# Transposes inside the key products, grad_out products in M's PSUM buffers, and two norms of the turn on ScalarE

## The chip, the cores and the metric

The kernel runs on one NeuronCore of a Trainium2 chip. The core has five engines that run their own instruction streams in order and meet at semaphores: TensorE (PE, matrix products; its weight loads are shown apart as PEld), VectorE (DVE), ScalarE (ACT), GpSimd (POOL) and SyncE (SP), which here only issues transfers. ACT and POOL issue some transfers too. The metric is the device time of one execution in microseconds, taken as the median of several.

## The reference

One forward and one backward pass of a pre-LN block over x of 2048 rows and 640 columns (bf16), with 32 heads of 20 columns and an MLP 1728 wide:

```python
phi = lambda t: where(t > 0, t + 1, exp(t)) + 1e-6
q, k, v = split(layernorm(x) @ wqkv)               # 32 heads
kv, z   = phi(k).T @ v, sum(phi(k))                # per head
h       = x + ((phi(q) @ kv) / (phi(q) @ z + 1e-6)) @ wo
hn      = layernorm(h)
out     = h + (silu(hn @ w1) * (hn @ w3)) @ w2
```

The kernel returns `out` and the gradients of x, wqkv, wo, w1, w3 and w2 for a given `grad_out` (B_x enters as a constant and isn't used in the result).

## The kernel before

Everything is cut into 16 tiles of 128 rows (`ST`), and 640 columns into 5 chunks of 128 (`DT`); a product over 640 columns is done in two halves of 320. Nothing is planned by a scheduler: the pools run under a manual schedule, so on each engine and each transfer queue the instructions stand in the order in which the Python code calls them.

**The first stage** (lines 432 to 513) loads x, normalises each tile in place in `x_sb` (bn_stats on DVE, the inverse root as a `pow` on POOL at L154, the norm itself on DVE at L160, or on ACT at L165 for tiles 10, 12 and 14), and turns it into `pqT`: tiles 0 to 7 by TensorE transposes (`p1_tr`, L254) that ACT copies out of PSUM (L256), tiles 8 to 15 by transfers on SP (L247). The loop over t then makes, for tile t, the key product of ten matmuls (`p1_mm`, L260) into a PSUM buffer `big`, of which there are two; `phi` takes it out with an Exp and a Relu on ACT (L277, L278) and two more steps on DVE (`rest`, L281 and L282) that are held back and called later by `phi_rest`. Key tile after key tile the loop also does the statistics of later tiles (`stat_of`), their norms (`norm_of`), four query products (`q_tile`), four products with grad_out (`ghh_chunk`, L371, which use one of the two `big` buffers), and the products of M = phi(k)^T x (`m_part`, L402, PSUM tags `m` and `tr`). In front of all that stand 44 products of a constant tile of ones (`warm`, L441), whose result nothing reads.

**The turn** (the `run(...)` at lines 801 to 809) stands between the end of the attention part and the MLP. `f2_half(t, j)` makes one half of h for tile t (L586, for t < 4 and j = 1 with a first product L584 that adds x), takes it out of PSUM (on DVE at L591 for j = 0, on ACT at L589 for j = 1) and takes its statistics on DVE; the second half also does the aggregation (L150), adds epsilon (L153) and asks POOL for the inverse root (L154). `f2_hn(t)` normalises on DVE (L160) into `hn`, and `f2_ht(t)` transposes it on TensorE (L677) and copies it out on ACT (L678). `mlp_ghh` is one more chunk of grad_out's products, taken out on ACT (L391).

**The backward loop** (L1112 to L1143) makes, for each row tile t, the 54 products of `b_ghn` (L1000): weights are 27 chunks of `ggb[t // 2]`, which holds two row tiles and has two buffers. The first 28 of the 54 products use chunks 0 to 13 and the operand `w13a`, the other 26 use chunks 14 to 26 and `w13b`. `load_gg` loads a `ggb` on the SP queue in two transfers: chunks 0 to 13 at even t, chunks 14 to 26 at odd t, for the pair of tiles that begins at the next even t. Within t the ACT queue issues a transposing transfer of the gradient of tile t - 1 (`b_gT`, L1037), then for t up to 10 one of `wo` or `kvT` (L1133). `b_gr(t - 2)` (L1057) uses the transposed gradient.

Of the kernel before, what the change touches and what calls it, by code (L numbers as in the profile page):

```python
# [9 lines left out]
P = 128  # L10
# [14 lines left out]
HD = D // 2  # L25
# [30 lines left out]
def kernel(  # L56
# [73 lines left out]
    class Stats:  # L130
# [31 lines left out]

        def norm_act(self, out, src, t):

            A.activation(out=out, in_=src, func=AF.Identity, bias=self.nb[t][:, 1:2], scale=self.rs[:, t:t + 1])  # L165

        def bias(self, t):
            nb = self.nb[t] = cp.tile([P, 2], F32, name="nb", bufs=4)
            G.tensor_tensor(out=nb[:, 0:1], in0=self.mv[:, t, 0:1], in1=self.rs[:, t:t + 1], op=ALU.mult)
            G.tensor_tensor(out=nb[:, 1:2], in0=zero[:], in1=nb[:, 0:1], op=ALU.subtract)  # L170

    ln1, ln2 = Stats("ln1"), Stats("ln2")

# [7 lines left out]
    def load_wq(a, b):  # L181
        dma(out=wqkv[:, :, a * HD:b * HD], in_=wq_v[:, :, a * HD:b * HD])

    def load_x(a, b):
        dma(out=x_sb[:, a:b, :], in_=xS[:, a:b, :])

    load_x(1, 2)
    A.activation(sg[:], zero[:], AF.Exp)
    load_wq(2, 3)
    load_wq(3, 4)  # L190
    load_x(2, 3)
    load_x(3, 4)
    load_x(4, 8)

# [40 lines left out]
    Z = cp.tile([P, DT], F32, name="Z")  # L235

    XT_DMA = 8
    WARM = 44

    def on_act(t):  # L240
        return t > XT_DMA and t % 2 == 0

    def p1_norm(t):
        xn = x_sb[:, t, :]
        (ln1.norm_act if on_act(t) else ln1.norm)(xn, xn, t)
        if t >= XT_DMA:
            dmaT(out=pqT[:, :, t * P:(t + 1) * P], in_=xn)  # L247

    def p1_tr(t, parts=((0, DT),)):
        xn = x_sb[:, t, :]  # L250
        for a, b in parts:
            tr = ps.tile([P, DT, P], BF16, name="tr", bufs=2)
            for c in range(a, b):
                T.transpose(tr[:, c, :], xn[:, c * P:(c + 1) * P], ident[:])  # L254

            A.copy(out=pqT[:, a:b, t * P:(t + 1) * P], in_=tr[:, a:b, :])  # L256

    def p1_half(acc, t, n0):
        for c in range(DT):
            T.matmul(acc, lhsT=pqT[:, c, t * P:(t + 1) * P], rhs=wqkv[:, c, n0:n0 + HD], start=(c == 0),  # L260
                     stop=(c == DT - 1))

    def p1_mm(t, n0):
        acc = ps.tile([P, 2, 512], F32, name="big", bufs=2)
        for j in range(2):
            p1_half(acc[:, j, 0:HD], t, n0 + j * HD)
        return acc

    def two(ap):
        return ap.rearrange("p (j n) -> p j n", j=2)  # L270

    held = []

    def phi(acc, dst, then=None):

        mq, rq = (p1.tile([P, D], BF16, name=n, bufs=b) for n, b in (("mq", 3), ("rq", 3)))
        A.activation(two(mq[:]), acc[:, :, 0:HD], AF.Exp)  # L277
        A.activation(two(rq[:]), acc[:, :, 0:HD], AF.Relu)  # L278

        def rest():  # L280
            V.tensor_scalar(out=mq[:], in0=mq[:], scalar1=1.0, scalar2=1e-6, op0=ALU.min, op1=ALU.add)  # L281
            V.tensor_tensor(out=dst, in0=mq[:], in1=rq[:], op=ALU.add)  # L282
            if then is not None:
                then()
        held.append(rest)

    def phi_rest(keep=0):
        while len(held) > keep:
            held.pop(0)()
# [13 lines left out]

    def q_tile(t):
        q_home(t)
        phi(p1_mm(t, 0), pqs[t])

    dz = {}

# [119 lines left out]
    def load_w2T(a, b):  # L429
        dmaT(out=w2T[:, :, a:b], in_=B_w2[a:b, :])  # L430

    zero_pads()
    load_w2T(0, 2 * P)
    load_g2T(0)
    load_w2T(2 * P, 4 * P)
    load_x(8, 12)
    load_wq(0, 2)
    load_x(12, ST)
    warm = ps.tile([P, 512], F32, name="warm", tag="tr", bufs=2)
    for _ in range(WARM):  # L440
        T.matmul(warm[:, 0:P], lhsT=ones[:], rhs=ones[:], start=True, stop=True, skip_group_check=True)  # L441
    ln1.run(x_sb, 0, 1)
    ln1.part(x_sb, 1, 0)
    for a, b in ((0, 2 * P), (2 * P, D)):
        ln1.norm(x_sb[:, 0, a:b], x_sb[:, 0, a:b], 0)
    p1_tr(0, ((0, 2), (2, DT)))
    for t in (1, 2):
        if t == 1:
            ln1.part(x_sb, t, 1)
            p1_norm(t)  # L450
            ln1.run(x_sb, t + 1, t + 2)
        else:
            ln1.part(x_sb, t + 1, 0)
            p1_norm(t)
    ln1.part(x_sb, 3, 1)
    w13 = [go for c0, c1 in ((0, 2), (2, 4), (4, 5)) for go in load_w13(c0, c1)]
    w13 += [lambda: dma(out=w1[:, :, F:FP], in_=rows(B_w3)[:, :, F - FL:F])]

    def load_wo():
        dma(out=wo[:], in_=A_wo.rearrange("(c p) n -> p c n", p=P))  # L460

    trickle = {3: w13[0], 4: w13[1], 11: lambda: load_wq(4, 6), 12: w13[2], 14: w13[3], 15: load_wo}

    stat_of = {t: (t + 4,) for t in range(7)}
    stat_of.update({7: (11, 12), 8: (13,), 9: (14,), 10: (15,)})
    norm_of = {t: (t + 3,) for t in range(8)}
    norm_of.update({8: (11, 12), 9: (13,), 10: (14,), 11: (15,)})

    def xn_out(g, q):
        sl = slice(g * TPC, (g + 1) * TPC)  # L470
# [5 lines left out]

    outs = {6: ((group_out, 0),), 7: ((xn_out, 0, dma),), 10: ((group_out, 1), (xn_out, 1, dma)), 13: ((group_out, 2),)}

    QT = (5, 7, 9, 11)
    for t in range(ST):  # L480
        k = p1_mm(t, D)
        if t < 3:
            p1_tr(t + 1, ((0, 2), (2, DT)))
        for n in stat_of.get(t, ()):
            ln1.run(x_sb, n, n + 1)
            if on_act(n):
                ln1.bias(n)
        for n in norm_of.get(t, ()):
            if not on_act(n):
                p1_norm(n)  # L490
        phi_rest(t < 4)
        phi(k, pk_all[:, t, :])
        for n in norm_of.get(t, ()):
            if on_act(n):
                p1_norm(n)
# [12 lines left out]
        for f, *n in outs.get(t, ()):  # L508
            f(*n)
        if t in trickle:  # L510
            trickle[t]()
# [285 lines left out]
    def kv3():  # L797
# [129 lines left out]

    ggb = {}

    def load_gg(j, c0, c1):  # L930
        if c0 == 0:
            ggb[j] = ba.tile([P, NG, 2 * P], BF16, name="ggb", bufs=2)
        dma(out=ggb[j][:, c0:c1, :],
            in_=gg_d[c0 * P:c1 * P, j * 2 * P:(j + 1) * 2 * P].rearrange("(c p) w -> p c w", p=P))

    def gw2_tail():
# [175 lines left out]
    for t in range(ST):  # L1112
        g = b_ghn(t)

        def part():
            next(g, None)

        u = t - 2
        if 2 <= t <= ST - 3:
            load_gg(t // 2 + 1, *((FT, NG) if t % 2 else (0, FT)))  # L1120
        part()
        part()
        part()
        if t + 2 < ST:
            b_load(t + 2)
        if t >= 1:
            ln_rest.pop(t - 1)()
            if by_dma(t - 1):
                b_gT(t - 1)
            if t <= 2 * DT:  # L1130
                n = (t - 1) % DT
                dst, src = (woT, A_wo) if t <= DT else (kvN, kvT_d)
                A.dma_start_transpose(out=dst[:, :, n * P:(n + 1) * P], in_=src[n * P:(n + 1) * P, :])  # L1133
# [300 lines left out]
```

## Time and profile before

| what | value |
|---|---|
| median of 6 runs | 826.96 us (826.25 to 828.49) |
| the profiled execution: its time, its span | 827.03 us, 825.3 us |
| TensorE busy | 815.5 us, 99% of the span |
| DVE, ACT, POOL busy | 453.6, 319.0, 133.9 us |
| granted TensorE clock | 0.999 |
| first stage: first warm product, first key product | 1.12 us, 6.92 us |
| the turn: first f2_half to first MLP product | 88.54 us to 101.68 us |
| the backward loop: first and last tile start | 404.6 us, 532.3 us |

The span runs from the first to the last instruction of the program; the execution's own time is 1.7 us longer. A line of a timeline has start, duration, engine, source line, operation, what it writes and reads, and in brackets the idle time of the engine before it with what ended it. TensorE shows as busy nearly throughout, so the time can change only by what makes TensorE wait, by products added or taken away, and by what lies ahead of its first useful product.

### The profile page before, as it was taken

How to read it: one execution, taken by the hardware profiler on the slowest of the kernel's cores; microseconds unless marked ns; L12 is line 12 of the kernel's file. 1: busy time of each engine (PE TensorE's matmuls, PEld its weight loads, DVE VectorE, ACT ScalarE, POOL GpSimd, SP SyncE). 2: the span in 40 equal slices, each digit the busy share in tenths (PEclk: the TensorE clock that was granted, in tenths of full speed). 3: DMA queues.
4: the chain of work that ended last, by engine and by line, in shares of the span. 5: the costliest groups of instructions: out<-in, count | busy, mean ns of one | idle time of the engine just before them, and what ended most of it. 6: DMA issues, size and time to landing. Idle time of an engine off the chain costs nothing.

```text
span 825.3 us, 14190 instructions
## 1 busy us (share of the span) xinstructions
PE 815.5 (99%) x5524; PEld 523.2 (63%) x5551; DVE 453.6 (55%) x960; ACT 319.0 (39%) x609; POOL 133.9 (16%) x196
## 2 busy tenths in 40 slices
PE   8999999999999999999999999999999999999998
PEld 5677644555555555777777777777777777555554
DVE  7859897899898566300057777772681545200000
ACT  5865787665655666011121222222212334211111
POOL 2335333323222212100001111110220000000000
PEclk9999999999999999999999999999999999999999
DMA  9899999696494455999878898358995788885771
GB/s 247 221 314 212 257 237 280 206 233 169 123 220 132 148 197 167 209 258 258 224 166 181 186 218 199 64 107 177 267 218 95 164 196 168 216 203 131 164 170 38
DMA packets 318338, 157.58 MB, mean 191 GB/s; under 512 B 235456, under 2 KB 311456, under 8 KB 318272
## 3 DMA queue, kind: packets, MB, share of 16 engines
q1 hardware_dynamic: 286256, 120.65, 63.4%
q0 software_dynamic: 7376, 24.81, 8.8%
q10 hardware_dynamic: 24640, 11.23, 6.8%
q8 instruction: 43, 0.70, 0.4%
q14 instruction: 23, 0.19, 0.1%
HBM read 48.15 MB, written 51.46 MB: 121 GB/s over the span
## 4 chain that ended last, share of the span: by engine, by line
PE 96%; DMA 2%; SPq 1%; ACT 0%; issue 0%; DVE 0%; POOL 0%; ACTq 0%
PE mm L371 20%; PE job L1198 19%; PE ghn L1000 14%; PE gxn L1356 8%; PE o L766 7%; PE gw L955 7%; PE big L260 3%; PE gwo L1085 3%; PE dkv L1302 3%; PE gr L1057 3%; PE macc L402 3%; PE at L586 2%; PE mm L260 1%; DMA pqT<-pql 1%; DMA g2T<-in_grad_out_dram 1%; PE dkv L1230 1%
## 5 line engine op out<-in xcount | busy, mean ns | idle before, releaser
L1198 PE MATMUL job<-gb,hnN 128*128 128x432 bf16 (+2 forms) x656 | 117.0, 342 | 0.0
L1000 PEld LDWEIGHTS <-ggb 128*128 128x128 bf16 x864 | 84.5, 98 | 32.8
L1198 PEld LDWEIGHTS <-hnN 128*128 128x128 bf16 x656 | 63.6, 98 | 53.4
L371 PE MATMUL mm<-pqT,w 128*128 128x512 bf16 x395 | 92.8, 379 | 0.4
L371 PEld LDWEIGHTS <-w 128*128 128x128 bf16 x540 | 52.5, 98 | 62.9 <-issue 0.8
L1202 ACT CAST obs<-job 128x432 bf16<-128x432 f32 (+3 forms) x61 | 29.3, 480 | 123.1 <-PE job L1198 120.7
L766 PE MATMUL o<-w,hhT 128*128 128x320 bf16 x448 | 67.6, 299 | 0.1
L1000 PE MATMUL ghn<-w13a,ggb 128*128 128x320 bf16 x448 | 63.5, 299 | 0.0
L1000 PE MATMUL ghn<-w13b,ggb 128*128 128x320 bf16 x416 | 61.4, 299 | 0.0
L371 PE MATMUL mm<-g2T,w2T 128*128 128x512 bf16 x229 | 58.9, 379 | 0.6
L766 PEld LDWEIGHTS <-hhT 128*128 128x128 bf16 x448 | 43.8, 98 | 23.6
L955 PE MATMUL gw<-g,hb 128*128 128x320 bf16 x416 | 56.8, 299 | 0.0
L1065 POOL TENSOR_TENSOR sz<-Zb,g_h 128x640 f32<-128x640 bf16 x16 | 20.2, 1261 | 199.3 <-DVE g_h L1063 199.3
L955 PEld LDWEIGHTS <-hb 128*128 128x128 bf16 x416 | 40.6, 98 | 16.0 <-issue 0.3
L1356 PE MATMUL gxn<-wqT,gT 128*128 128x320 bf16 x320 | 48.7, 299 | 0.0
L391 ACT CAST ghh<-mm 128x512 bf16<-128x512 f32 x48 | 28.2, 587 | 47.5 <-PE mm L371 42.0
L705 ACT ACTIVATE sig<-mm 128x512 bf16<-128x512 f32 x56 | 33.5, 598 | 27.8 <-PE mm L371 25.0
L1012 ACT ACTIVATE gs<-ghn 128x640 bf16<-128x640 f32 x16 | 11.2, 703 | 79.0 <-PE ghn L1000 79.0
L260 PE MATMUL big<-wqkv,pqT 128*128 128x320 bf16 x260 | 39.3, 299 | 1.8 <-DMA wqkv<-in_A_wqkv_dram 1.1
L371 PEld LDWEIGHTS <-w2T 128*128 128x128 bf16 x260 | 25.3, 98 | 24.6 <-issue 1.3
L260 PEld LDWEIGHTS <-pqT 128*128 128x128 bf16 x320 | 30.6, 98 | 14.6 <-ACT pqT L256 1.8
L1356 PEld LDWEIGHTS <-gT 128*128 128x128 bf16 x320 | 31.3, 98 | 12.2
(201 smaller groups left out, 1282.4 us busy)
## 6 DMA issues: line engine op xcount, KB each, us to landing
hh_d<-hhT SPq DMA_DIRECT2D x24, 256.0 KB, 2.6
gg_d<-gate POOLq DMA_DIRECT2D x24, 256.0 KB, 4.0
gg_d<-ghh POOLq DMA_DIRECT2D x24, 256.0 KB, 3.4
ggb<-gg_d SPq DMA_DIRECT2D x6, 896.0 KB, 5.8
ggb<-gg_d SPq DMA_DIRECT2D x6, 832.0 KB, 7.6
x_sb<-in_A_x_dram SPq DMA_DIRECT2D x7, 640.0 KB, 7.0
out_dram<-obs ACTq DMA_DIRECT2D x39, 108.0 KB, 3.0
ggb<-gg_d SPq DMA_DIRECT2D x2, 1728.0 KB, 13.4
```

Source lines behind the costliest of these rows:

```text
L260: T.matmul(acc, lhsT=pqT[:, c, t * P:(t + 1) * P], rhs=wqkv[:, c, n0:n0 + HD], start=(c == 0), stop=(c == DT - 1))
L371: T.matmul(acc[:], lhsT=w[:, c, fc * P:(fc + 1) * P], rhs=rhs[:, c, :], start=(c == 0), stop=(c == DT - 1))
L391: A.copy(out=ghh[n // 2][:, n % 2, :], in_=acc[:])
L402: T.matmul(macc[m][j][:, 0:n], lhsT=pk_all[:, t, m * P:(m + 1) * P], rhs=x_ext[:, t, j * HD:j * HD + n], start=(t == 0), stop=(t == ST - 1))
L705: A.activation(sig[:, i, :], gp[:], AF.Sigmoid)
L766: T.matmul(o2["ps"][:, 0:HD], lhsT=hhT[c][:, fc, i * P:(i + 1) * P], rhs=w2[:, fc, j * HD:(j + 1) * HD], start=(fc == 0), stop=(fc == FT - 1))
L955: T.matmul(acc[:, j, 0:HD], lhsT=hb[b][:, t, i * P:(i + 1) * P], rhs=g2[:, t, j * HD:(j + 1) * HD], start=(t == 0), stop=(t == ST - 1))
L1000: T.matmul(acc[:, j, 0:HD], lhsT=ggb[t // 2][:, k, lo:lo + P], rhs=rhs[:, j * HD:(j + 1) * HD], start=(k == 0), stop=(k == NG - 1))
L1057: T.matmul(gr[t][:, j, 0:HD], lhsT=ghT[t][:, c, :], rhs=wT2[:, c, j * HD:(j + 1) * HD], start=(c == 0), stop=(c == DT - 1))
L1198: T.matmul(acc[:, 0:n], lhsT=lhs[:, t, m * P:(m + 1) * P], rhs=rhs(t), start=(t == 0), stop=(t == ST - 1))
L1202: A.copy(out=ob, in_=acc[:, 0:n])
L1356: T.matmul(acc[:, j, 0:HD], lhsT=g, rhs=wqT[:, k, j * HD:(j + 1) * HD], start=(k == 0), stop=(k == 14))
```

## The change

In the first stage, tile 0 is only centred at first (its first 256 columns on DVE, the others on ACT with a bias of minus the mean); the scale is put into the Exp and Relu of its key and query products (`RAW = 1`), and `p1_scale` scales the tile in `x_sb` at t = 3. The transposes of tile t + 1 stand between the two halves of key product t, each tile with one copy. The warm products are 34, in M's buffers, and 8 more follow the transposes of tile 0. The loop's DVE work follows a written list (`v_steps`). Chunks of grad_out's products stand at t = 3 to 6 instead of 2 to 5 and use the two buffers `m`, so M's first products begin at t = 7. The first query product moves from t = 5 to t = 6. The load of x's tile 2 stands ahead of the second half of the key weights, that of tiles 8 to 11 ahead of w2's second part. The bias of ACT's norms is one POOL instruction instead of two. In the turn, the first half of tile 2 stands ahead of the second halves of tiles 0 and 1, and the norms of tiles 1 and 2 are done on ACT. In the backward loop the second half of each `ggb` is issued on the ACT queue, after `b_gT`.

```diff
         def norm_act(self, out, src, t):
-            A.activation(out=out, in_=src, func=AF.Identity, bias=self.nb[t][:, 1:2], scale=self.rs[:, t:t + 1])
+            A.activation(out=out, in_=src, func=AF.Identity, bias=self.nb[t][:, 0:1], scale=self.rs[:, t:t + 1])
         def bias(self, t):
-            nb = self.nb[t] = cp.tile([P, 2], F32, name="nb", bufs=4)
-            G.tensor_tensor(out=nb[:, 0:1], in0=self.mv[:, t, 0:1], in1=self.rs[:, t:t + 1], op=ALU.mult)
-            G.tensor_tensor(out=nb[:, 1:2], in0=zero[:], in1=nb[:, 0:1], op=ALU.subtract)
+            nb = self.nb[t] = cp.tile([P, 1], F32, name="nb", bufs=4)
+            G.tensor_scalar(out=nb[:], in0=self.mv[:, t, 0:1], scalar1=self.rs[:, t:t + 1], scalar2=-1.0, op0=ALU.mult,
+                            op1=ALU.mult)
...
     load_wq(2, 3)
+    load_x(2, 3)
     load_wq(3, 4)
-    load_x(2, 3)
     load_x(3, 4)
...
-    WARM = 44
+    WARM = 34
+    RAW = 1
...
+    def p1_scale(t):
+        xn = x_sb[:, t, :]
+        V.tensor_scalar(out=xn, in0=xn, scalar1=ln1.rs[:, t:t + 1], scalar2=None, op0=ALU.mult)
...
-    def p1_mm(t, n0):
+    def p1_mm(t, n0, between=None):
         acc = ps.tile([P, 2, 512], F32, name="big", bufs=2)
         for j in range(2):
             p1_half(acc[:, j, 0:HD], t, n0 + j * HD)
+            if j == 0 and between is not None:
+                between()
         return acc
...
+        kw = dict(scale=ln1.rs[:, t:t + 1]) if t < RAW else {}
+        A.activation(two(mq[:]), acc[:, :, 0:HD], AF.Exp, **kw)
+        A.activation(two(rq[:]), acc[:, :, 0:HD], AF.Relu, **kw)
...
     load_g2T(0)
+    load_x(8, 12)
     load_w2T(2 * P, 4 * P)
-    load_x(8, 12)
...
+    def warm_up(n):
+        warm = ps.tile([P, 512], F32, name="warm", tag="m", bufs=2)
+        for _ in range(n):
+            T.matmul(warm[:, 0:P], lhsT=ones[:], rhs=ones[:], start=True, stop=True, skip_group_check=True)
+    warm_up(WARM)
...
+    def center_first():
+        V.tensor_scalar(out=nmean[:], in0=ln1.mv[:, 0, 0:1], scalar1=-1.0, scalar2=None, op0=ALU.mult)
+        center(0, 0, 2 * P)
+        A.activation(out=x_sb[:, 0, 2 * P:], in_=x_sb[:, 0, 2 * P:], func=AF.Identity, bias=nmean[:, 0:1])
...
+    ln1.part(x_sb, 0, 0)
+    ln1.part(x_sb, 0, 1, center_first)
     p1_tr(0, ((0, 2), (2, DT)))
+    warm_up(8)
+    stat(1)
+    ln1.part(x_sb, 2, 0)
+    p1_norm(1)
+    ln1.part(x_sb, 2, 1)
+    ln1.part(x_sb, 3, 0)
+    p1_norm(2)
     ln1.part(x_sb, 3, 1)
+    ln1.part(x_sb, 4, 0)
+    p1_norm(3)
+    ln1.part(x_sb, 4, 1)
...
-    trickle = {3: w13[0], 4: w13[1], 11: lambda: load_wq(4, 6), 12: w13[2], 14: w13[3], 15: load_wo}
+    trickle = {4: w13[0], 5: w13[1], 11: lambda: load_wq(4, 6), 12: w13[2], 14: w13[3], 15: load_wo}
+    R = None
+    v_steps = {1: (R, ("N", 4)), 2: (("S", 5), R, ("N", 5)), 3: (("S", 6), R, ("N", 6), ("C", 0)),
+               4: (("S", 7), R, ("N", 7), ("S", 8)), 5: (R, ("N", 8), ("S", 9)), 6: (R, ("N", 9), ("S", 10)),
+               7: (("S", 11), R, R, ("A", 10), ("N", 11)), 8: (("S", 12), R, R, ("S", 13), ("A", 12)),
+               9: (("N", 13), R, ("S", 14)), 10: (R, R, ("S", 15), ("A", 14)), 11: (("N", 15), R)}
+    V_OPS = {"S": stat, "N": p1_norm, "C": p1_scale}
...
-    QT = (5, 7, 9, 11)
+    QT = (6, 7, 9, 11)
+    M0 = {7: (0, 1, 2), 8: (3, 4, 5)}
+    M0.update({t: (t - 3,) for t in range(9, ST)})
     for t in range(ST):
-        k = p1_mm(t, D)
-        if t < 3:
-            p1_tr(t + 1, ((0, 2), (2, DT)))
...
+        k = p1_mm(t, D, (lambda: p1_tr(t + 1)) if t + 1 < XT_DMA else None)
+        steps = v_steps.get(t, (R,) * len(held))
+        for step in steps:
+            if step is R:
+                held.pop(0)()
+            elif step[0] != "A":
+                V_OPS[step[0]](step[1])
+        phi(k, pk_all[:, t, :], t)
+        for step in steps:
+            if step is not R and step[0] == "A":
+                p1_norm(step[1])
         if t in QT:
             q_tile(QT.index(t))
-        if 2 <= t < 6:
-            ghh_chunk(t - 2, ps.tile([P, 2, 512], F32, name="gp", tag="big", bufs=2)[:, 0])
-            p1_tr(t + 2)
-        if t >= 3:
-            m_part(0, [t - 3])
+        if 3 <= t < 7:
+            ghh_chunk(t - 3, ps.tile([P, 512], F32, name="gp", tag="m", bufs=2))
+        m_part(0, M0.get(t, ()))
...
-    def f2_hn(t):
+    def f2_hn(t, on_act=False):
...
-        ln2.norm(hn[t][:], x_sb[:, t, :], t)
+        if on_act:
+            ln2.bias(t)
+            ln2.norm_act(hn[t][:], x_sb[:, t, :], t)
+        else:
+            ln2.norm(hn[t][:], x_sb[:, t, :], t)
...
-        (sig_table,), (f2_half, 0, 0), (f2_half, 1, 0), (f2_half, 0, 1), (f2_half, 1, 1), (f2_hn, 0), (mlp_ghh, 5),
-        (f2_half, 2, 0), (f2_hn, 1), (load_w2T, 10 * P, F), (f2_half, 2, 1), (f2_ht, 0), (f2_half, 3, 0), (f2_hn, 2),
+        (sig_table,), (f2_half, 0, 0), (f2_half, 1, 0), (f2_half, 2, 0), (f2_half, 0, 1), (f2_half, 1, 1), (f2_hn, 0),
+        (mlp_ghh, 5), (f2_hn, 1, True), (load_w2T, 10 * P, F), (f2_half, 2, 1), (f2_ht, 0), (f2_half, 3, 0), (f2_hn, 2, True),
         (f2_half, 3, 1), (f2_ht, 1), (mlp_ghh, 6), (f2_hn, 3), (f2_ht, 2), (r_red, 6), (r_inv, 6), (r_scale, 6), (r_T, 6),
...
-        if 2 <= t <= ST - 3:
-            load_gg(t // 2 + 1, *((FT, NG) if t % 2 else (0, FT)))
+        if 2 <= t <= ST - 3 and t % 2 == 0:
+            load_gg(t // 2 + 1, 0, FT)
...
             if by_dma(t - 1):
                 b_gT(t - 1)
+            if 2 <= t <= ST - 3 and t % 2:
+                load_gg(t // 2 + 1, FT, NG, A.dma_start)
```

More of the change, by code (lines that the diff above doesn't have):

```diff
@@ L272, with phi @@
     held = []
-    def phi(acc, dst, then=None):
+    def phi(acc, dst, t):
         mq, rq = (p1.tile([P, D], BF16, name=n, bufs=b) for n, b in (("mq", 3), ("rq", 3)))
-        A.activation(two(mq[:]), acc[:, :, 0:HD], AF.Exp)
-        A.activation(two(rq[:]), acc[:, :, 0:HD], AF.Relu)
+        kw = dict(scale=ln1.rs[:, t:t + 1]) if t < RAW else {}
+        A.activation(two(mq[:]), acc[:, :, 0:HD], AF.Exp, **kw)
+        A.activation(two(rq[:]), acc[:, :, 0:HD], AF.Relu, **kw)
         def rest():
@@ L282, in rest @@
             V.tensor_tensor(out=dst, in0=mq[:], in1=rq[:], op=ALU.add)
-            if then is not None:
-                then()
         held.append(rest)
@@ L305, in q_tile @@
         q_home(t)
-        phi(p1_mm(t, 0), pqs[t])
+        phi(p1_mm(t, 0), pqs[t], t)
     dz = {}
@@ L434, with center, stat @@
     load_g2T(0)
+    load_x(8, 12)
     load_w2T(2 * P, 4 * P)
-    load_x(8, 12)
     load_wq(0, 2)
     load_x(12, ST)
[L439 to L445, printed above, removed]
-    p1_tr(0, ((0, 2), (2, DT)))
[L447 to L454, printed above, removed]
+    def warm_up(n):
[3 more added lines that the diff above has]
+    warm_up(WARM)
+    def center(t, a=0, b=D):
+        ln1.center(x_sb[:, t, a:b], x_sb[:, t, a:b], t)
+    nmean = cp.tile([P, 1], F32, name="nmean")
+    def center_first():
+        V.tensor_scalar(out=nmean[:], in0=ln1.mv[:, 0, 0:1], scalar1=-1.0, scalar2=None, op0=ALU.mult)
+        center(0, 0, 2 * P)
+        A.activation(out=x_sb[:, 0, 2 * P:], in_=x_sb[:, 0, 2 * P:], func=AF.Identity, bias=nmean[:, 0:1])
+    def stat(t):
+        ln1.run(x_sb, t, t + 1)
+        if on_act(t):
+            ln1.bias(t)
+    ln1.part(x_sb, 0, 0)
+    ln1.part(x_sb, 0, 1, center_first)
+    p1_tr(0, ((0, 2), (2, DT)))
+    warm_up(8)
[5 more added lines that the diff above has]
+    p1_norm(2)
     ln1.part(x_sb, 3, 1)
+    ln1.part(x_sb, 4, 0)
+    p1_norm(3)
+    ln1.part(x_sb, 4, 1)
     w13 = [go for c0, c1 in ((0, 2), (2, 4), (4, 5)) for go in load_w13(c0, c1)]
@@ L460, in load_wo @@
         dma(out=wo[:], in_=A_wo.rearrange("(c p) n -> p c n", p=P))
-    trickle = {3: w13[0], 4: w13[1], 11: lambda: load_wq(4, 6), 12: w13[2], 14: w13[3], 15: load_wo}
[L464 to L467, printed above, removed]
+    trickle = {4: w13[0], 5: w13[1], 11: lambda: load_wq(4, 6), 12: w13[2], 14: w13[3], 15: load_wo}
[5 more added lines that the diff above has]
+    V_OPS = {"S": stat, "N": p1_norm, "C": p1_scale}
     def xn_out(g, q):
@@ L477 @@
     outs = {6: ((group_out, 0),), 7: ((xn_out, 0, dma),), 10: ((group_out, 1), (xn_out, 1, dma)), 13: ((group_out, 2),)}
-    QT = (5, 7, 9, 11)
+    QT = (6, 7, 9, 11)
+    M0 = {7: (0, 1, 2), 8: (3, 4, 5)}
+    M0.update({t: (t - 3,) for t in range(9, ST)})
     for t in range(ST):
-        k = p1_mm(t, D)
-        if t < 3:
-            p1_tr(t + 1, ((0, 2), (2, DT)))
[L484 to L495, printed above, removed]
+        k = p1_mm(t, D, (lambda: p1_tr(t + 1)) if t + 1 < XT_DMA else None)
[9 more added lines that the diff above has]
+                p1_norm(step[1])
         if t in QT:
             q_tile(QT.index(t))
-        if 2 <= t < 6:
-            ghh_chunk(t - 2, ps.tile([P, 2, 512], F32, name="gp", tag="big", bufs=2)[:, 0])
-            p1_tr(t + 2)
-        if t >= 3:
-            m_part(0, [t - 3])
+        if 3 <= t < 7:
+            ghh_chunk(t - 3, ps.tile([P, 512], F32, name="gp", tag="m", bufs=2))
+        m_part(0, M0.get(t, ()))
         if t >= 11:
@@ L928, with load_gg @@
     ggb = {}
-    def load_gg(j, c0, c1):
+    def load_gg(j, c0, c1, q=dma):
         if c0 == 0:
             ggb[j] = ba.tile([P, NG, 2 * P], BF16, name="ggb", bufs=2)
-        dma(out=ggb[j][:, c0:c1, :],
+        q(out=ggb[j][:, c0:c1, :],
             in_=gg_d[c0 * P:c1 * P, j * 2 * P:(j + 1) * 2 * P].rearrange("(c p) w -> p c w", p=P))
```

## The prediction

> **What bounds the kernel now.** The page's first part, then the waits of TensorE:
>
> ```profile
> PE 815.5 (99%) x5524; PEld 523.2 (63%) x5551; DVE 453.6 (55%) x960; ACT 319.0 (39%) x609; POOL 133.9 (16%) x196
> ...
> PE big L260 <- DMA wqkv<-in_A_wqkv_dram: 1.1, 2, 0.8
> PE gp L371 <- DMA g2T<-in_grad_out_dram: 1.0, 1, 1.0
> PE trh L677 <- DVE hn L160: 0.8, 1, 0.8
> PE big L260 <- ACT pqT L256: 0.6, 2, 0.3
> PE at L586 <- DMA Wp<-pkx: 0.3, 1, 0.3
> ```
>
> Behind the first product at 6.92 TensorE idles some 3 us in 818, all in two places: the first 15 us, and the turn. No list of waits shows one in the backward loop. So the diff can win at most 3 us, and its third part can only lose. These idle times count from the modelled end of the matmul before; from start to start less the normal pitch the turn's two are 0.98 and 0.45.
>
> The chain into the turn's wait, from the timelines of TensorE, DVE, POOL:
>
> ```profile
> 97.97 0.84 PE L586 MATMUL at<-Wp,pqT 128*128 128x320 bf16 x5
> 99.63 0.45 PE L677 MATMUL trh<-ident,hn 128*128 128x128 bf16 x5 [0.81 <-DVE hn L160]
> ...
> 97.54 0.49 DVE L147 BATCH_NORM_STATS2 st<-x_sb 128x6 f32<-128x320 bf16 x1
> 98.06 0.21 DVE L150 BATCH_NORM_AGGREGATE ln_mv<-st 128x2 f32<-128x12 f32 x1
> 98.31 0.15 DVE L153 TENSOR_SCALAR ln_ve<-ln_mv 128x1 f32<-128x1 f32 x1
> 99.13 0.45 DVE L160 TENSOR_SCALAR hn<-x_sb,ln_mv,ln_rs 128x640 bf16<-128x640 bf16 x1 [0.66 <-POOL ln_rs L154]
> ...
> 98.54 0.55 POOL L154 TENSOR_TENSOR ln_rs<-ln_ve,mhalf 128x1 f32<-128x1 f32 x1 [1.56 <-DVE ln_ve L153]
> ```
>
> From a second half's statistics to a finished norm is 2.0 us of latency (97.54 to 99.58), whichever engine norms.
>
> For the backward loop, the queues of SP and ACT and TensorE's timeline around row tile 4:
>
> ```profile
> 423.12 0.42 SPq L933 DMA_DIRECT2D ggb<-gg_d  x1
> 436.85 0.38 SPq L933 DMA_DIRECT2D ggb<-gg_d  x1
> ...
> 432.95 1.22 ACTq L1037 DMA_TRANSPOSE ghT<-g_h  x1
> 434.21 1.30 ACTq L1133 DMA_TRANSPOSE woT<-in_A_wo_dram  x1
> ...
> 436.66 3.97 PE L1000 MATMUL ghn<-w13a,ggb 128*128 128x320 bf16 x28
> 440.46 1.25 PE L1000 MATMUL ghn<-w13b,ggb 128*128 128x320 bf16 x8
> ```
>
> The load at 423.12 is the second half for tiles 4 and 5: needed at 440.46, issued 17 us ahead.
>
> **What the skill says.** "TensorE: Matmul & The Clock Gate", the section on the architectural detail of Part 1, has ACT and DVE as strict FIFOs. The timelines agree: each ACT instruction stands in the order of the code. So a norm on ACT that waits for POOL holds every later PSUM copy. The same page ("What you observe") has cold products 107 ns apart and warm ones 56: the warm products here start 0.107 us apart until 5.04 and 0.056 from 5.15. "DMA: Bandwidth & Descriptors" (Issuing engines are not separate DMA queues) says that transfers of different engines share the same 16 DMA engines and another issuer saves only issue time. The page agrees in that SP's 12 loads of ggb take a median 6.5 us (5.5 to 8.4), longest where ACT's transposes mix with them.
>
> **The change, part by part.** I worked each engine forward in its program order, from the rows' durations. The same working of the kernel before puts the end of the first stage's loop within 0.2 us of the trace, and the turn's end at 101.8 (traced 101.7).
>
> *Start.* Centring earlier brings the transposes of tile 0 to 4.8 from 5.53, but product 0 waits for wqkv (landed 6.88, the first idle time above), so this is worth nothing. The 42 warm products end before that: nothing. Should the clock rise late, key products cost 0.27 instead of 0.136 each, about 1 us; TensorE has 0.7 us of room before product 10 (below), so 0.3 would remain. Tile 2's load (0.45 us of transfer, its landing less the one before) passes wqkv's second half, which lands at 8.47 instead of 8.02; but tile 1's transposes, now ahead of that half, wait too: their norm stands on DVE behind tile 2's statistics, which wait for that load (7.33), so 8.28. Product 0 with transposes ends at 9.2, before 9.0: +0.2.
>
> *Key products 1 to 4.* ACT has per tile a copy (0.61), Exp and Relu (0.60 each) against 1.64 on TensorE, so about 0.3 of waiting remains at products 1, 2 and 3. What goes is g2T's wait (1.0): its chunk comes after product 3, at 15.0, and it landed at 14.7. TensorE reaches product 10 at 35.1, before 36.8: 1.7 ahead.
>
> *Where that goes.* DVE is busy 4.4 to 4.6 of each 5 us here, and the new list puts the norms of tiles 12 and 14 on ACT ahead of the Exp and Relu of products 9 and 11, which free the `big` buffer that products 10 and 12 need. Statistics 12 end at 32.45, POOL's power 33.15, bias 33.6, norm (0.92, L165) 34.5, Exp and Relu to 35.8: product 10 waits 0.7. Likewise statistics 14 end at 38.6, norm at 40.7, Relu of product 11 at 41.9: product 12 starts at 41.96, before 42.5. So 0.5 is left, and less if DVE has a pause as before (0.5 at 23.43); and tile 15's transfer, in the queue behind two stores of 640 KB, lands at about 48.5 just as product 15 comes, so it may hold too. I take −0.2; ends −0.7 (bias at 0.19, L170's row) and +0.7 (bias 0.7, transposing transfers 0.4 later).
>
> *Turn.* TensorE: a half is 0.68 (0.81 with x), a chunk 1.08, a tile's transposes 0.28. With tile 2's half ahead, the second halves start at 90.58, after Wp (landed 90.44): −0.45. But DVE now has that half's copy and statistics (0.94) ahead of tile 0's: norm 0 ends at 94.37, its transposes come at 94.42 instead of 94.10: +0.32. Tile 1: statistics 93.09, epsilon 94.00, power 94.63, bias 95.0, norm on ACT 95.05 to 95.97. Behind it on ACT stands the copy of half (2,1), which left TensorE at 94.27: it ends at 96.28. So tile 2's chain starts at 96.3: epsilon 97.23, power 97.86, bias 98.24, norm on ACT 98.28 to 99.20, transposes at 99.25 where TensorE is at 97.55: +1.70. Behind that norm on ACT stands the copy of half (3,1), to 99.51: statistics 99.55, power 101.09, norm on DVE 101.58, transposes at 101.63 where TensorE is at 100.21: +1.42, before 0.98. Sum 0.32 + 1.70 + 1.42 − 0.98 − 0.45 = **+2.0**. What DVE saves (two norms of 0.36) doesn't count: it waits for ACT. The bias's form isn't in this trace; at 0.19 or 0.7 instead of 0.3 the sum is 1.8 or 2.8. If the evacuations were not held, it would be near −1.2.
>
> *Backward loop.* The second halves are issued behind ghT's transpose, so at 434.2 instead of 423.1: 11 us later. A first half alone (436.85) landed after 5.5 us; so 439.7, against 440.46: 0.8 of room. At the median, 6.5, it is 0.3 late; with woT's transposes behind it and the next first half (436.85) beside it, up to 8.1 as at 440.97: 1.9 late. Six loads (t = 3 to 13): 0, 2 or 11 us. ACT's issue (0.4) is hidden, as its next computing instruction (gs) waits until 436.86; woT's transpose behind it moves by 0.4 and is needed only after the loop. SP loses six issues of 0.43, and what stood behind them (the loads of hnb) waits for buffers until 430.96 anyway. I take +0.4.
>
> *Moves that I cost at nothing.* Grad_out's chunks in M's buffers are each copied out within 1.2 us of their end, and M's first product comes after, at t = 7; p1_scale (0.36 on DVE) is in the working above. The load of x's tiles 8 to 11 passes a transposing load of w2, which then lands at some 18.5 (15.99 before): its chunk comes at 20.5. The first query product, one tile later, comes at 23.3; its weights landed at 22.36. The first loads of w1 and w3 move a tile later and are first read at 101.7. On SP tile 11's transposing transfer now stands ahead of tile 10's, which lands near 35.2; product 10 waits until 35.8 anyhow, but without that cover it costs 0.1.
>
> Sum: −0.2 + 2.0 + 0.4 = +2.2 on a span of 825.3 and an execution of 827.03: 829.2. The median lay 0.07 below that execution, nothing here.
>
> **Rivals.**
> 1. *The loads of ggb come late.* For: 0.8 us of room, transposes on the same queue, six times. Against: SP has nothing else under way until 436.85. At 1 us each for six: 827.0 + 1.8 + 6 = 835.
> 2. *A wash.* The turn's loss 1.6, the first stage's gain 0.7, the loads in time: 827.9. For: most intervals in the turn are chains of four engines, where 0.1 each adds up. Against: the holding copies are plain in the order.
> 3. *Faster.* Norm 1 on ACT is ready before half (2,1) ends, that is by 94.3 instead of 95.97: then no copy is held, the turn gives −1.2 and with the first stage −0.7: 825.1. It decides at tile 1's bias: ready by 93.4 instead of 95.0. POOL issues transfers until 93.17 and has two powers of 0.55 to do first, which speaks against it.
>
> **How the numbers follow.** A measurement tells 0.2% (1.65 us) from no change. Forecast (turn loses, loads at most 2 us late in all): 0.50. Rival 1, over that: 0.20. Rival 2, within 0.2%: 0.21. Rival 3, faster: 0.09. Slower 0.70, same 0.21, faster 0.09. The likeliest case alone runs from 828.6 to 831. The range leaves out the faster case and the far end of rival 1: 827.3 to 833.5.
>
> **What would show it.** In TensorE's waits: no L371 on g2T, no L586 on Wp; trh waits of about 1.7 and 1.4 on hn, released by ACT for tile 2, with the ACT copies L589 of halves (2,1) and (3,1) directly after the two norms; big waits near 35 and 42 on ACT's Relu. In the loop, either no ghn wait or one at the first product on w13b of each even tile. The prediction is wrong if the copies are not held, if TensorE passes product 12 more than a microsecond earlier than before, or if ghn waits add up to more than 2 us.

## The result and the profile after

The changed kernel takes 831.85 us (median of 21 executions, 828.74 to 837.76), the kernel before 827.02 in the same runs (42 executions): a ratio of 1.0059 [1.0045, 1.0074], so slower by 4.8 us in the median. (The ratios here and below weigh all executions, so a tail shows in them that a median can hide; in brackets stands their 95% interval.) The profiled execution took 830.06 with a span of 828.3 (before 827.03 and 825.3). The forecast was 829.2, with a range of 827.3 to 833.5.

The page's first part (busy time, share, instructions by engine):

```profile
PE 816.5 (99%) x5522; PEld 522.4 (63%) x5549; DVE 452.6 (55%) x959; ACT 321.7 (39%) x609; POOL 133.6 (16%) x195
```

Four lines of TensorE's waits (us in total, times, longest; `trh` is what `f2_ht` writes, `ghn` what `b_ghn` writes, `big` what the key and query products write):

```profile
PE trh L703 <- ACT hn L165: 1.6, 1, 1.6
PE trh L703 <- DVE hn L160: 1.3, 1, 1.3
...
PE big L265 <- DMA pqT<-x_sb: 0.7, 1, 0.7
...
PE ghn L1026 <- DMA ggb<-gg_d: 0.4, 1, 0.4
```

The waits on g2T and Wp are gone from the list. In their place stand two in the turn, one in the first stage for a transposing transfer, and one in the loop where before there was none. The turn in TensorE's timeline (start, length, idle before it and what ended that):

```profile
97.81 0.45 PE L703 MATMUL trh<-ident,hn 128*128 128x128 bf16 x5 [1.63 <-ACT hn L165]
...
100.19 0.71 PE L703 MATMUL trh<-ident,hn 128*128 128x128 bf16 x5 [1.25 <-DVE hn L160]
100.70 2.34 PE L377 MATMUL mm<-g2T,w2T 128*128 128x512 bf16 x5
```

In ACT's, with the two norms and the copies of halves (2,1) and (3,1):

```profile
93.62 0.92 ACT L165 ACTIVATE hn<-x_sb,nb,ln_rs 128x640 bf16<-128x640 bf16 x1 [0.97 <-POOL nb L169]
94.45 0.40 ACT L611 CAST x_sb<-at 128x320 bf16<-128x320 f32 x1
...
96.83 0.92 ACT L165 ACTIVATE hn<-x_sb,nb,ln_rs 128x640 bf16<-128x640 bf16 x1 [1.39 <-POOL nb L169]
97.66 0.41 ACT L611 CAST x_sb<-at 128x320 bf16<-128x320 f32 x1
```

In DVE's, the statistics behind the first of these copies:

```profile
94.88 0.49 DVE L147 BATCH_NORM_STATS2 st<-x_sb 128x6 f32<-128x320 bf16 x1 [2.07 <-ACT x_sb L611]
```

And in POOL's, the bias of tile 1:

```profile
93.33 0.26 POOL L169 TENSOR_SCALAR nb<-ln_mv,ln_rs 128x1 f32<-128x1 f32 x1
```

ACT waits for POOL's bias, norms, and only then copies the half that left TensorE long before; DVE's statistics wait for that copy, and at the end of the chain TensorE waits. TensorE's row at 100.70 shows something else: five products of 512 columns take 2.34 us instead of 1.24. The granted clock by stretches (columns: length, then busy time and count of PE, PEld, DVE, ACT and POOL, then clock, DMA share, GB/s):

```profile
92.72:96.13 3.41, 3.33 (x26) 2.01 (x26) 1.27 (x5) 1.82 (x3) 1.01 (x3) 1.00 1.08 368
96.13:99.55 3.41, 1.18 (x11) 0.69 (x10) 1.42 (x5) 2.71 (x5) 1.01 (x3) 1.00 1.15 304
99.55:102.96 3.41, 2.77 (x11) 1.39 (x12) 3.13 (x8) 0.88 (x2) 0.11 (x1) 0.50 1.22 266
```

The records have the clock at half from 99.546 for 3.413 us. In the stretch of that length just before, which holds the first wait and 0.6 us of the second, TensorE was busy 1.18 us.

To compare traces I measure four stretches on TensorE: product 0 to the first product of the turn (L608), from there to the first product of the MLP, to the first ghn product, and through fifteen sixteenths of the ghn products.

| kernel profiled | product 0 starts | to the turn | turn | MLP | loop |
|---|---|---|---|---|---|
| before | 6.92 | 81.62 | 13.14 | 302.92 | 127.68 |
| after | 5.83 | 81.24 | 16.51 | 303.05 | 128.61 |

The change is −1.09 − 0.38 + 3.37 + 0.13 + 0.93 = +2.96, against +3.0 between the spans. What this pair doesn't explain is the median, 1.8 us above the profiled execution, and the times up to 837.8.

### The profile page after: what moved, and what is told of

The parts are those of the page before. It is cut to its first block, busy times and chain, and to the rows that moved or that the text cites. A ratio compares the mean times of both kernels' runs of the same rounds, so it can differ in the third digit from the quotient of the medians.

```text
span 828.3 us, 14193 instructions
## 1 busy us (share of the span) xinstructions
PE 816.5 (99%) x5522; PEld 522.4 (63%) x5549; DVE 452.6 (55%) x959; ACT 321.7 (39%) x609; POOL 133.6 (16%) x195
## 4 chain that ended last, share of the span: by engine, by line
PE 80%; DVE 3%; ACTq 2%; DMA 2%; issue 1%; ACT 1%; POOL 0%
PE mm L377 20%; PE job L1226 19%; PE ghn L1026 8%; PE gxn L1384 8%; PE o L792 7%; PE gw L981 7%; PE gwo L1111 3%; PE dkv L1330 3%; PE at L608 2%; PE gr L1083 2%; DMA ggb<-gg_d 2%; ACTq L1161 1%; DVE wb L1041 1%; PE dkv L1258 1%; ACT gs L1038 1%
```

## The experiments

Theory: the copies held behind ACT's norms are the loss, and the loop adds some tenths. Rivals: the first stage brings the loss or its spread; the late loads do.

### The three parts, each alone

`first_only` takes the hunks of the first stage, `turn_only` those of the turn (with the shorter bias), `loop_only` those of the backward loop; the rest is the kernel before. `turn_fill` is `turn_only` with products into a spare buffer, whose results nothing reads, where TensorE would wait (the calls that change, cut out of longer lines):

```diff
-(mlp_ghh, 6), (f2_hn, 3), (f2_ht, 2),
+(mlp_ghh, 6), (f2_hn, 3), (fill_pe, 26), (f2_ht, 2),
-(f2_half, 4, 0), (f2_ht, 3), (mlp_ghh, 7),
+(f2_half, 4, 0), (fill_pe, 22), (f2_ht, 3), (mlp_ghh, 7),
```

> Only the turn's part (and the shorter bias), the rest as before. Theory A: TensorE waits 1.7 and 1.3 us for the two last norms, 2 us more than before, and the waits bring the granted clock to one half for a stretch of 3.4 us, which costs another 1 to 1.7: 3 to 4 us slower in the median, and a spread of some 4 us, because where the stretch falls changes from execution to execution. Rival C (waits alone, the clock's fall is an accident of the profiled execution): 2.0 slower with a spread as before. Rival D (the loop is the larger cost): under 2 us.

> The turn's part as in turn_only, with 26 products of the tile of ones (1.5 us) ahead of the transposes of tile 2 and 22 (1.2 us) ahead of those of tile 3, in the places where TensorE waits; their result isn't used. Theory A: the waits stay but the clock doesn't fall: 1.8 to 2.3 us slower than before, and 1 to 1.7 faster than turn_only, with a spread as before. Rival C: like turn_only, within 0.5 us.

> Only the backward loop's part: the second halves of ggb on the ACT queue. Theory A: the loads land 5.5 to 6.8 us after their issue with 6 us of room, so 0.5 to 1 us slower in the median and up to 3 in some executions. Rival D: 2 to 4 us slower in the median and the larger part of the changed kernel's spread, since the profiled execution, with 0.9 us lost in the loop, was among the fast ones. Rival E: same as before, hidden.

> Only the first stage's part of the change (with POOL's shorter bias), the turn and the backward loop as before. Theory A (the turn and the loop lose, the first stage wins): 1.3 to 1.7 us faster than before, as the changed kernel's trace reaches the turn at 87.07 instead of 88.54; executions within 3 us of each other. Rival B (the first stage is a source of the changed kernel's loss or of its spread): same or slower than before, or executions that differ by more than 4 us. By the prediction's own sum the gain would be 0.2.

Measured against a median of 826.72 of the kernel before:

| kernel | median us (range, executions) | ratio |
|---|---|---|
| turn_only | 830.61 (828.70 to 831.63, 6) | 1.0041 [1.0028, 1.0053] |
| turn_fill | 828.99 (828.23 to 830.68, 11) | 1.0028 [1.0020, 1.0037] |
| loop_only | 827.36 (826.57 to 828.94, and one at 840.71 that isn't in the ratio, 21) | 1.0008 [1.0002, 1.0015] |
| first_only | 834.46 (826.17 to 836.78, 22) | 1.0061 [1.0037, 1.0085] |

*Turn.* In `turn_only` the turn takes 16.53 us, as with the whole change (16.51), and the clock falls at 100.89, again for 3.413 us. In `turn_fill` TensorE works through the waits:

```profile
99.78 1.39 PE L787 MATMUL fill<-ones 128*128 128x128 bf16 x22
101.19 0.45 PE L681 MATMUL trh<-ident,hn 128*128 128x128 bf16 x5
101.48 1.24 PE L371 MATMUL mm<-g2T,w2T 128*128 128x512 bf16 x4
```

The clock stays up (1.24 us again in the last row) and the turn takes 15.17: 2.03 more than before. The products added don't lengthen it: the last transposes start 13.12 us after the turn's first product, as in the trace after. So the 3.4 us are 2.0 of held copies and 1.35 of clock. The clock doesn't fall in every execution: the two of `turn_only` with a mean clock of 0.999 or above took 828.70, the other four 830.6 to 831.6.

*Loop.* Its stretch takes 128.20, 0.52 more than before; the one wait shown is this, on the last of the six loads moved:

```profile
527.66 1.26 PE L1000 MATMUL ghn<-w13b,ggb 128*128 128x320 bf16 x8 [0.34 <-DMA ggb<-gg_d]
```

That load took 6.70 us from issue to landing, the other five 5.5 to 5.7.

*First stage.* This I had not expected. Of 22 executions seven lie from 826.17 to 827.83, one at 830.14 and fourteen from 833.1 to 836.8. The profiled one took 835.1. Its rows in the turn, whose code is that of before, first in TensorE's timeline:

```profile
105.25 0.71 PE L699 MATMUL trh<-ident,hn 128*128 128x128 bf16 x5 [7.55 <-DVE hn L160]
```

in DVE's:

```profile
104.75 0.45 DVE L160 TENSOR_SCALAR hn<-x_sb,ln_mv,ln_rs 128x640 bf16<-128x640 bf16 x1 [7.61 <-DMA pqT<-pql]
```

and in that of SP's queue (start and length of the issue):

```profile
88.87 1.33 SPq L367 DMA_TRANSPOSE pqT<-pql  x1
90.25 11.42 SPq L436 DMA_TRANSPOSE w2T<-in_B_w_dram  x1
```

DVE had the statistics of row tile 3 at 97; its norm waits until 104.75 for a transfer. The code says why: for tiles 2 and 3 `f2_hn` allocates `hn` under the tag `pql` (four buffers), so hn of tile 3 is written into the pql buffer of tile 5, whose last reader is the transposing transfer issued at 88.87. It landed at 104.62. From 99.79, within the wait of 7.55 us, the clock is at half for 10.24 us. In the trace of before the same transfer stands as

```profile
89.96 1.33 SPq L361 DMA_TRANSPOSE pqT<-pql  x1
```

and landed at 97.42, 1.7 us before hn of tile 3 could be written.

The three medians don't add up to the whole change: alone the parts cost 7.7, 3.9 and 0.6 us. One reason is in the traces. In the changed kernel the held copies put the norm of tile 3 at 99.69, 12.62 us into the turn; with the first stage alone and the buffer out of the way (`first_own`, below) it comes 10.59 into it. A late transfer of tile 5 so costs the changed kernel some 2 us less. How often it's late there isn't known: in its one trace it wasn't (7.4 us).

### Taking the buffer away, and the order without ACT's norms

Three kernels write hn of tile 3 into a slot of `pq` whose readers were done before the turn: `first_own` (with the first stage alone), `before_own` and `after_own`.

```diff
-        hn[t] = (pf.tile([P, D], BF16, name="hn", tag="pql", bufs=4) if 2 <= t < TPC else
+        hn[t] = (pq6[:, 0, :] if t == 3 else
+                 pf.tile([P, D], BF16, name="hn", tag="pql", bufs=4) if t == 2 else
```

`turn_order` is `turn_only` without its norms on ACT (again the calls alone):

```diff
-(f2_hn, 1, True), (f2_hn, 2, True)
+(f2_hn, 1), (f2_hn, 2)
```

> Only the first stage is changed (as in first_only), and hn of row tile 3 is written into a slot of pq that has long been read, instead of the pql buffer of tile 5, whose last reader is the transposing transfer issued at 88.9. Theory (that buffer is what the slow executions of first_only waited for, up to 7.6 us, and the clock fell in that wait): the trh wait is below 1 us, the spread closes, and the first stage's gain is left: median 825.3 to 826.4, at most one execution in ten above 829. Rival (the spread comes from the first stage itself, its few warm products or its loads): the median stays above 829, with executions of 826 and of 834 to 836 beside each other. Rival (the congestion of the transfers behind it delays something else as well): median between, 827 to 830.

> The kernel before with hn of row tile 3 in the same free slot of pq. In its trace the transposing transfer of tile 5 landed at 97.42 and the norm could start at 99.1 at the earliest, so the buffer is free in time in most executions. Theory: median unchanged, 826.4 to 827.0, and no execution above 829.5. Rival (the buffer costs the kernel before something in each execution): 825.0 to 826.2.

> The whole change with hn of row tile 3 in the free slot of pq. Theory (the tail of the changed kernel, 832 to 838 us, is the same wait for the same buffer; the held copies of the turn are not touched by it): lowest time as with the change (828.7), median 828.8 to 830.0, none above 832. Rival (the tail is the falling clock in the held copies' waits, or the late loads of the loop): median stays 831 to 832.5, with times up to 837.

> Of the turn only the new order is kept (the first half of tile 2 ahead of the second halves of tiles 0 and 1); the norms of tiles 1 and 2 stay on DVE. All else is the kernel before. Theory (the turn's loss comes from the copies that ACT holds behind the two norms): no copy of a half is held, the trh waits of 1.7 and 1.4 us go, and the time is that of before within a microsecond: 826.0 to 827.6. Rival (the order is what costs, since DVE gets the copy and statistics of tile 2's half before those of tile 0): 828 to 829.5, with the waits still there.

Measured against 826.82 of before:

| kernel | median us (range, executions) | ratio |
|---|---|---|
| first_own | 827.05 (825.97 to 831.53, 14) | 1.0003 [0.9984, 1.0021] |
| before_own | 826.55 (825.74 to 828.77, 14) | 0.9997 [0.9989, 1.0005] |
| after_own | 830.49 (829.00 to 831.43, 6) | 1.0040 [1.0026, 1.0054] |
| turn_order | 826.66 (826.00 to 827.49, 14) | 0.9999 [0.9991, 1.0006] |

`first_own` shows what the executions of `first_only` above 833 wait for: none of its 14 lies there, where `first_only` had 14 of 22. In its trace the transfer of tile 5 is late again, and it no longer matters. The transfer in its list of DMA issues (last the us from issue to landing):

```profile
pqT<-pql SPq DMA_TRANSPOSE x1, 13.9
```

and TensorE's wait for hn of tile 3:

```profile
PE trh L700 <- DVE pq L160: 0.6, 1, 0.6
```

(the free slot goes by the name pq). The clock stays up and the turn takes 13.14 us, as before. Two executions above 831 remain, and the median, 827.05, lies above the range of the theory, just within that of the second rival: the late transfers may hold something else now and then. No trace of those two was taken. `before_own` stayed in its range, so the buffer costs the kernel before nothing in most executions; whether its rare ones above 835 (one of 42 beside the changed kernel) are the same wait can't be told from 14. `after_own` has no execution above 831.43, where the changed kernel has ten of 21 above 832. That fits the same buffer as the cause of the change's tail, but doesn't show it: six executions are few, no trace of an execution in that tail was taken, and the median, 830.49, lies above the range on record. The rest of the loss stays, with the same trh waits (1.6 and 1.3) and the same fall of the clock.

`turn_order` shows that the order is free: its turn takes 12.79 us, 0.35 less than before, and ACT holds no copy. The one wait left in it is that of before, somewhat shorter:

```profile
98.52 0.45 PE L681 MATMUL trh<-ident,hn 128*128 128x128 bf16 x5 [0.67 <-DVE hn L160]
```

The turn's loss is the two norms on ACT: 2.4 us against this order without the clock (2.03 and 0.35). What a norm on ACT would give that holds no copy (−1.2 in the prediction) no run shows.

### What makes the transfer late

`first_late` was meant to take away the transposing load of w2 that SP issues right behind tile 5's transfer. By my mistake it moved the other part of w2, the one issued at 99, so that its expectation doesn't describe it. `first_late2` moves both. `best` puts together the first stage, the order of `turn_order` and the free slot; `best_late_own2` is `best` with both loads of w2 moved. The move in `first_late2`, the calls alone:

```diff
-(q_out, 10, 14), (load_w2T, 8 * P, 10 * P), (mlp_ghh, 4),
+(q_out, 10, 14), (mlp_ghh, 4),
-(f2_hn, 1), (load_w2T, 10 * P, F), (f2_half, 2, 1),
+(f2_hn, 1), (f2_half, 2, 1),
-(f2_hn, 3), (f2_ht, 2),
+(f2_hn, 3), (load_w2T, 8 * P, 10 * P), (f2_ht, 2),
-(r_T, 6),
+(r_T, 6), (load_w2T, 10 * P, F),
```

> Only the first stage is changed (as in first_only, hn of row tile 3 again in the pql buffer of tile 5), and the transposing load of w2 that SP issued at 90.3, right behind the transposing transfer of tile 5, stands behind the store of hn of row tile 3, some 9 us later. Theory (the transfer of tile 5 lands at 103 to 105 instead of 96 to 97 because that load and POOL's four stores are under way beside it): without the load it lands by 96.5, the trh wait is below 1 us and no execution lies above 830: median 825.8 to 826.8. Rival (POOL's stores alone delay it, or something ahead of it in its queue): it still lands after 100 in many executions, and the median stays above 829 with times up to 836.

> The first stage of the change, the turn in the new order with all norms on DVE, hn of row tile 3 in the free slot of pq, the loop as before. Theory (first_own lacks 0.3 us of gain only because of executions with late transfers; turn_order costs nothing; the parts add up): median 826.0 to 827.0, the same as before. Rival (earlier halves let the whole gain of the first stage, 0.3 us, and 0.4 of the turn through): 825.2 to 826.0, faster by 0.1 to 0.2%. Rival (late transfers of w2 or of the stores hold something else in the turn): 827 to 829 with executions above 830.

> As first_late was meant: there the part of w2 that moved was the one issued at 99, not the one issued at 90.3 right behind the transposing transfer of tile 5. Here both move: the transposing load of two blocks of w2 stands behind the store of hn of row tile 3, the load of the rest behind the next transposing transfer. First stage of the change, turn and loop as before, hn of row tile 3 in the pql buffer of tile 5. Theory (the two kinds of transfer, transposing loads of w2 and POOL's stores, congest each other in some executions, and tile 5's transfer is caught in it): with the load gone it lands by 96 in the trace, and no execution lies above 830: median 825.9 to 826.8. Rival (POOL's stores alone, or tile 5's transfer itself, make the congestion): executions at 834 to 836 remain, two in six or more.

> First stage of the change, turn in the new order with norms on DVE, hn of row tile 3 in the free slot of pq, loop as before, and both loads of w2 later as in first_late2. Theory (in best the executions above 830 were the same congestion, whose next victim was the buffer of gate, held by a late store): all executions between 825.3 and 827.5, median 825.6 to 826.3, faster than before by up to 0.1%. Rival (the late loads of w2 hold grad_out's products of chunks 8 to 13, or the congestion remains): median 827 or more.

Measured, each against before in the same runs (826.46, 826.46, 826.75, 826.75):

| kernel | median us (range, executions) | ratio |
|---|---|---|
| first_late | 826.62 (826.04 to 835.59, 6) | 1.0033 [0.9998, 1.0067] |
| best | 826.19 (825.49 to 831.12, 6) | 1.0003 [0.9986, 1.0020] |
| first_late2 | 828.19 (826.19 to 833.29, 22) | 1.0020 [1.0000, 1.0040] |
| best_late_own2 | 826.45 (825.66 to 827.46, 22) | 0.9991 [0.9980, 1.0001] |

`first_late` is in effect a repeat of `first_only`: four executions at 826.0 to 826.7 and two at 834.5 and 835.6. Its profiled execution is one of the quick ones. There tile 5's transfer landed 7.2 us after its issue, and TensorE waited 0.6. Its median hides the two, its ratio doesn't.

`first_late2` contradicts the theory as I had written it, and its rival, with executions at 834 to 836, didn't come either. With no load of w2 under way until 100.98, the transfer still took 11.3 us (88.66 to 100.01) and TensorE waited 3.1. Ten of its 22 executions lie above 829. So the lateness doesn't need w2's load. That load may make the lateness worse: the worst time is 3.5 us lower than in `first_only`, and the transfer took 13.9 to 15.9 us in the three late traces with that load.

In the profiled execution of `best` (831.12) the transfer was late, with hn safe. The next to be held was a buffer of `gate`, a tile of the MLP, that an equally late store of POOL still read. TensorE's waits have:

```profile
PE mm L377 <- ACT gate L734: 3.3, 1, 3.3
```

and ACT's timeline:

```profile
117.98 0.59 ACT L734 CAST gate<-mm 128x512 bf16<-128x512 f32 x1 [3.56 <-DMA gg_d<-gate]
```

`best_late_own2` has no execution above 827.46 where the 43 of before reach 836.35. That doesn't prove the tail gone: before has only four of its 43 above 829. Its median lies 0.15 above the range on record, and its ratio can't tell it from the kernel before, so no version here is shown to beat that.

*What sets the late traces apart.* POOL issues a store (to `m_d`) right after SP issues tile 5's transfer. The fourteen traces sorted by how long after:

| m_d's issue after the transfer's | traces | the transfer took |
|---|---|---|
| 0.23 to 0.41 us | 10 (all without the first stage, after, after_own, first_late, best_late_own2) | 7.0 to 7.6 us |
| 0.02 to 0.10 us | 4 (first_only, first_own, best, first_late2) | 11.3 to 15.9 us |

No trace lies between. In the late ones little moves for a time. A window of 3 us of before (length, clock, DMA share, GB/s):

```profile
94.00:97.00 3.00, 1.00 1.13 276
```

and the same of first_only:

```profile
94.00:97.00 3.00, 1.00 0.85 64
```

In this window the four late traces moved 64 to 214 GB/s, the other ten 276 to 404.

The traces offer a second mark that sorts them as well. SP's load of x and POOL's first store (to `r_d`) are issued just before this pair. In the four late traces the store lands 0.2 to 0.6 us before the load, in the other ten 0.5 to 0.6 after it. So the queues may have changed places one transfer earlier.

With the first stage SP has less time in hand. In the trace of before it ends the transfers of Wp at 89.02 and issues the load of x at 89.47, for 0.38 us; in `first_only` it ends at 88.14 and issues that load at 88.20, for 0.56 us, with POOL's first store issued 0.11 after (before 0.18). That alone doesn't decide: the four quick traces with the first stage have the same 0.06 and 0.56. In three of the four late ones the last transfer of Wp took 1.35 to 1.41 us to issue instead of 1.2, and SP's issues slipped by that much; in `best` it took 1.21. That nearness makes the transfer late is a correlation over fourteen traces. No run moves SP's issue alone, so the cause inside the queues stays open, and so does why x's load takes longer to issue.

## Why the prediction was right, and where its sum was short

*Turn.* Right in mechanism and size. Predicted: bias of tile 1 at 95.0, waits of 1.70 and 1.42, sum +2.0. In the trace after the turn begins 1.47 earlier; with that added the bias ends at 95.06. The waits, counted from start to start as there, are 1.58 and 1.41 (1.63 and 1.25 in the list), and with the clock up the sum is +2.03 (`turn_fill`). The faster rival fell where it said it would: the bias came 1.7 us too late. One line of the prediction is wrong, though its working is right: the latency from statistics to norm is not 2.0 us whichever engine norms. Through ACT it's 2.9 for tile 2 (94.88 to 97.75), with the bias and a norm of 0.92 instead of 0.45.

*The term that was missing* is the clock: I priced the two waits as idle time alone. Two waits within one stretch of 3.41 us cost another 1.35. "TensorE: Matmul & The Clock Gate", in the section Why this matters for your kernels, warns of idle gaps over about 3 us. Here no gap was longer than 1.63, but TensorE idled 2.2 of 3.41 us, and the clock fell; the measurement decides.

*First stage.* Taken at −0.2. From product 0 to the turn the eight profiles with it have a median of 81.24 us, the six without it 81.64. The earlier start, which I had costed at nothing, is worth something as well: the working assumed the key weights at 6.88. Those landed anywhere from 5.54 to 6.88 in the fourteen profiles, whatever stood in the queue, and product 0 started 0.04 us later with the new start (0.32 in one), but on average 0.39 later with the old. The turn starts at 87.54 on average instead of 88.11: −0.6, within the ends given. The times show less of it. The seven executions of `first_only` below 828 have a median of 826.59 against 826.72 of before, so how much of the 0.6 is left at the end stays open. The −1.09 of the first pair of profiles was mostly such a landing. In the trace after, product 10 came 28.9 us after product 0, as worked out, but by luck: the trace names the transposing transfer of tile 10 behind tile 11's, which I had seen as covered. The wait for ACT's Relu at product 12 didn't come. That product started 1.92 us earlier than before, 0.83 when counted from product 0, so the sign given for a wrong prediction (more than a microsecond earlier) appeared by the letter. Later tile 15's transfer held product 15 by 0.3, as the working allowed for.

*The step that failed* is that the turn's transfers were taken as they stood. The working followed TensorE, ACT, DVE and POOL, but named hn's statistics as the only thing that its norm waits for, and not the buffer it is written into. In the trace of before that buffer had been free for 1.7 us. An earlier turn and a later landing both eat that reserve, and by their times it was gone in 14 of 22 executions of `first_only`. The changed kernel's median is 4.8 us above before, that of `after_own` 3.7. By that difference, an estimate from six executions, the late transfer is worth some 1.1 in it.

*Loop.* +0.4 taken; the stretch is longer by 0.93, 0.52 and 0.11 in the three profiles with it. The late-loads rival fell: landings took 5.4 to 6.8 us from ACT's queue against 0.8 us of room on 5.5, late in at most two loads of six, by some tenths (0.3 and 0.6 in the trace after).

The median is +4.8 where +2.2 was forecast: about 2.0 of held copies, 1.35 of clock, 0.5 of the loop, −0.6 of the first stage, and 1.1 of the late transfer make 4.4. The two of the turn are shown by runs, the last two are estimates. The sign was right, and the time lay in the range because its upper end had been put out for late loads in the loop, which was not the reason: that part was luck.

## What to carry to other kernels

Before moving an operation to an engine that works in strict order, look at what stands behind it there: a norm that is cheap by its busy time cost its whole wait for POOL, twice. When something is brought forward, list for each instruction not only its inputs but the last reader of the buffer it writes; a transfer that landed 1.7 us early in one trace is no reserve. Compare stretches between fixed points, not whole profiles: a first load that lands a microsecond earlier looks like a gain of the change.

## What was not expected of the hardware

The clock fell to half for 3.413 us after stretches of that length in which TensorE was still busy for a third of the time, transposes included (idle 2.2 to 2.3 us in three traces, 2.1 in a fourth; in two more it was idle for over 3). Of the other such stretches, laid end to end before and after a fall, those with up to 1.5 us idle kept the clock. None at full clock had between 1.5 and 2.1 us, so where between them the limit lies isn't known. And one transposing transfer took 7.0 to 7.6 us or 11.3 to 15.9 us, apart by whether another queue's store was issued more than 0.2 us behind it or up to 0.1. Why is open.
